# A convolution stem with all its gradients on one core: the order of all engines planned anew, with transfer times by kind and stage

## The chip, the cores and the metric

The kernel runs on one NeuronCore of a Trainium2 chip. The metric is device time in microseconds (us) of one execution. The five engines are TensorE (PE, matmuls), VectorE (DVE), ScalarE (ACT), GpSimd (POOL) and SyncE (SP). SP's and POOL's work here is mostly the issue of DMA transfers, which 16 DMA engines then carry out.

## The reference

A strided convolution over time, a normalisation over time in each channel, a tanh-gelu, and the gradients of everything for a given gradient of the output, all in bfloat16:

```python
def _fwd_reference(x, w, gn_gamma, gn_beta):   # x: 2 x 16000 x 256, w: 31 x 256 x 256
    s = 2
    L = (T - K) // s + 1                        # 7985
    h = jnp.einsum('blc,cd->bld', x[:, 0:s * L:s, :], w[0])
    for i in range(1, K):
        h = h + jnp.einsum('blc,cd->bld', x[:, i:i + s * L:s, :], w[i])
    mu = jnp.einsum('bld->bd', h)[:, None, :] / L
    var = jnp.einsum('bld->bd', (h - mu) ** 2)[:, None, :] / L
    h = (h - mu) / jnp.sqrt(var + 1e-5)
    h = h * gn_gamma[None, None, :] + gn_beta[None, None, :]
    return _gelu(h)

def reference(x, w, gn_gamma, gn_beta, grad_out):
    ...
    _out, _vjp = jax.vjp(_f, x, w, gn_gamma, gn_beta)
    _grads = _vjp(grad_out)
    return (_out0, *[jnp.asarray(_g) for _g in _grads])
```

The outputs are out_0 (the gelu), out_1 (the gradient of x), out_2 (of w), out_3 and out_4 (of gamma and beta).

## The kernel before

The convolution is taken apart twice into three branches each, A, B and C, with sums and differences of phases of x (on DVE) and of taps of w, so that fewer matmuls are needed than 31 taps would ask for. PE's work runs in five stages, in this order of time:

- **F0** and **F1**, the forward convolution of the first and the second image (matmuls of `f_mm`, L736), each in four chunks of time. The sums of x are `tt` in `f_sums` (L694), the results leave the accumulators in `f_evac`.
- **G0** and **G1**, the gradient of x (matmuls of `g_mm`, L1324), again in four chunks for each image. G0 holds the three chunks of the first image and the start of the fourth, G1 the rest. For every chunk `e_load` loads what the gelu's backward pass left (tensors dyd) and the forward result (hd); `e_comp` turns them into the gradient of the convolution's output with two scalings (L1206 for hd, L1208 for dyd), a sum (L1217) and four copies (`spread`, L1226, on ACT); `g_sums` takes the differences `first`, `second` and `third` (all L1277) that the matmuls read. `g_three_b` computes a part once, and an ACT copy (L1351) puts it into the second half of the accumulator, where `g_three_ac` adds to it. `g_seed` (L1385, or `keep`, L831) and `g_evac` (L1395) move accumulators. `dl_turn` transposes the differences by DMA (L549) and stores them to the tensors dld for the last stage. In the same stretch as G0's first half the gelu's backward pass of the second image runs on ACT and DVE (`gelu_unit`: L1096 and L1098, L1101, L1103 and L1105, L1107, L1111, L1122, L1124).
- **W**, the gradient of w (matmuls of `w_mm`, L1528), in nine combinations of branches. Each loads planes of x (`x_raw`, 1 MB each, tensor in_x_dram), sums them (`w_add`, L1496), loads the tensors dld (`d_tile`), and takes sums and differences of pairs (`pair_x`, L1598; `pair_d`, L1614; `leaf_d`, L1699).

Nothing is issued as it is written. Every instruction, matmul group or transfer is handed to `Plan.add` with its engine, an estimated duration, and the memory that it reads and writes; from the latter come its predecessors. After the whole program is written, `order()` gives every entry a due time: the point of PE's own progress at which it is needed, less its duration, less a number from the table `lead` (by kind: stage, function and caller) and one from the table `fine` (by kind and part, the part being the chunk or combination). `listing()` then walks through time with a model of the five engines and of the DMA queues: whenever an engine is free it takes, among the entries that are ready, the one with the earliest due time. `emit()` issues everything in the order of the start times so found, and pins it. So these numbers alone decide in which order each engine runs its queue; each engine executes its queue strictly in this order, and an instruction that waits holds up all behind it.

A transfer enters the model with `dur`, the time of its issue on SP's queue, `dma`, the time that its packets take, and `ns`, the time of one packet, both worked out in `load` and `turn` from its size and the length of its runs:

```python
        pk = 8192 if run >= 4096 else 4096 if eng == "POOL" else run
        np_ = nbytes / pk
        ns = (PKS if out.space == bass.MemoryType.DRAM else PK)[pk]
        add(eng, {"POOL": 0.74, "SP": 0.46 + 0.00016 * np_, "ACT": 0.4}[eng], [out], [in_],
            lambda: e.dma_start(out=out, in_=in_), dma=np_ * ns / 16e3 * 1.03, ns=ns, tp=SH[pk], slack=slack)
```

The duration of an ACT instruction comes from `act(n)`, of a DVE instruction from `dve(n, rate)`, of a matmul from `mmt(n)`.

Of the kernel before, what the change touches and what calls it, by code (L numbers as in the profile page):

```python
# [30 lines left out]
def act(n, extra=0.0):  # L31
    return 0.06 + n * 0.00097 + extra
# [6 lines left out]
class Plan:  # L39
# [3 lines left out]
    def __init__(self, tc):  # L43
# [10 lines left out]
            "F0 f_evac last": 5.0,  # L54
            "F0 f_mm f_leaf": -288.0,
            "F0 f_mm f_outer": -149.5,
            "F0 f_mm f_three_ac": -4.5,
            "F0 f_mm f_three_b": -5.5,
            "F0 f_mm pe_turn": -527.0,
            "F0 f_outer forward": -46.0,  # L60
            "F0 f_seed forward": -48.5,
            "F0 f_three_b forward": -129.5,
            "F0 keep f_evac": 35.5,
            "F0 load conv_stem_kernel": -15.5,
            "F0 load f_evac": 42.5,
            "F0 tt f_sums": -120.5,
            "F0 tt second": 20.5,
            "F0 tt third": -36.0,
            "F0 turn w2_part": -3.0,
            "F0 turn x_load": -8.5,  # L70
            "F0 ve f_seed": -122.5,
            "F0 ve_neg f_seed": 49.0,
            "F0 w_sub f_first": -76.5,
            "F0 w_sum w2_part": -13.5,
            "F1 f_evac last": -106.5,
            "F1 f_mm f_leaf": -335.0,
            "F1 f_mm f_outer": 74.0,
            "F1 f_mm f_three_ac": -8.5,
            "F1 f_mm f_three_b": -75.5,
            "F1 f_three_b forward": -73.0,  # L80
            "F1 gelu_unit gelu_batch": -2.0,
            "F1 load gelu_unit": 23.0,
            "F1 load out0_store": 15.0,
            "F1 tt f_sums": -79.5,
            "F1 tt gelu_unit": -49.5,
            "F1 tt second": -38.0,
            "F1 tt third": -225.5,
            "F1 turn gelu_batch": 56.0,
            "F1 turn gelu_unit": -12.5,
            "F1 turn x_load": 35.5,  # L90
            "F1 w_sub f_again": 4.5,
            "G0 e_comp e_load": 0.5,
            "G0 g_evac last": 1.5,
            "G0 g_mm g_leaf": -24.5,
            "G0 g_mm g_outer": 22.0,
            "G0 g_mm g_three_ac": -0.5,
            "G0 g_mm g_three_b": -7.0,
            "G0 g_three_b input_grad": 4.5,
            "G0 gelu_unit gelu_batch": -7.0,
            "G0 keep g_evac": -281.0,  # L100
            "G0 keep g_seed": -15.0,
            "G0 load dl_turn": 2.5,
            "G0 load e_load": 41.0,
            "G0 load g_evac": 23.5,
            "G0 load gelu_unit": -7.0,
            "G0 spread e_comp": -1.0,
            "G0 tiny elem_finalize": -1.0,
            "G0 tt first": -111.5,
            "G0 tt second": -4.5,
            "G0 tt third": -12.5,  # L110
            "G0 turn dl_turn": 3.5,
            "G0 turn gelu_batch": -12.0,
            "G0 w_sum load_w2": -53.0,
            "G0 w_sum w2_outer": -11.5,
            "G1 cp e_comp": 13.5,
            "G1 e_comp e_load": 13.5,
            "G1 g_evac last": -0.5,
            "G1 g_mm g_outer": -7.5,
            "G1 g_mm g_three_ac": -9.0,
            "G1 g_mm g_three_b": -30.5,  # L120
            "G1 g_three_b input_grad": -66.0,
            "G1 keep g_seed": -132.0,
            "G1 load dl_turn": 11.0,
            "G1 load e_load": -8.0,
            "G1 load g_evac": 12.0,
            "G1 spread e_comp": -1.5,
            "G1 tt first": -1.0,
            "G1 tt second": -17.0,
            "G1 tt third": -86.5,
            "G1 turn dl_turn": 3.5,  # L130
            "G1 zero e_comp": -8.0,
            "W keep w_keep": -5.5,
            "W keep weight_grad": -31.0,
            "W leaf_d weight_grad": 0.5,
            "W load d_tile": -49.5,
            "W load out0_late": 165.0,
            "W load w_done": 3.0,
            "W load w_emit": 24.5,
            "W load weight_grad": 2.5,
            "W load x_raw": 1.0,  # L140
            "W pair_d weight_grad": -3.0,
            "W pair_x weight_grad": 1.0,
            "W turn out0_late": -38.0,
            "W ve w_done": 11.5,
            "W ve weight_grad": -24.0,
            "W w_add weight_grad": 2.5,
            "W w_add x_tile": 8.0,
            "W w_both weight_grad": 11.0,
            "W w_emit weight_grad": -234.0,
            "W w_mm w_leaf": -9.0,  # L150
            "W w_pairs weight_grad": -136.0,
# [3 lines left out]
        self.overlap = {"DVE": 0.084, "ACT": 0.1}  # L155
        self.fine = {
            "F0 f_evac last": {0: -191.0, 1: -57.0, 3: -4.0},
            "F0 f_mm f_outer": {0: 138.5, 2: 14.0},
            "F0 f_mm f_three_ac": {0: -41.0, 1: -74.0, 2: -68.0, 3: -25.5},
            "F0 f_mm f_three_b": {2: 96.5, 3: 55.0},  # L160
            "F0 f_mm pe_turn": {0: -106.0},
            "F0 f_outer forward": {0: 69.5},
            "F0 f_seed forward": {0: -15.0, 3: -58.5},
            "F0 keep f_evac": {1: -5.5, 2: -40.5, 3: -32.5},
            "F0 load f_evac": {0: -85.5, 3: 8.5},
            "F0 load put": {1: 170.5, 3: 1.0},
            "F0 load_gb conv_stem_kernel": {1: -70.0},
            "F0 tt f_sums": {1: 46.0, 3: 20.0},
            "F0 tt second": {0: 77.0, 1: -78.0, 2: 2.0, 3: -60.0},
            "F0 tt third": {0: 60.5, 1: -127.0, 2: 39.0, 3: -34.5},  # L170
            "F0 turn w2_part": {1: 3.0, 3: -18.0},
# [1685 lines left out]
```

## Time and profile before

| | |
|---|---|
| median of 3 runs | 1154.29 us (1152.07 to 1155.96) |
| profiled execution | 1154.13 us, span 1152.4 us |
| PE busy | 1122.5 us (97%), 7652 matmuls |
| DVE busy | 997.9 us (87%), 920 instructions |
| ACT busy | 532.7 us (46%), 817 instructions |
| POOL busy | 125.4 us (11%) |
| longest waits of PE | 4.7 and 4.5 us in the first 23 us, 3.4 us at 655 us, 2.8 us at 1006 us |

The span is the profiled execution from its first to its last instruction; the execution's own time holds 1.73 us more. Since PE is busy for 97% of it, a place matters where PE stands still, and the question at each such place is which engine's instruction it waits for, what stood ahead of that one in its engine's queue, and which transfer in turn held that. In a row of a timeline the numbers are the start in us from the beginning of the span, the duration, the engine, the line, the operation, what it writes and reads, and how many instructions are taken together; in brackets behind it stands the idle time of the engine just before it and what ended it. SPq is SP's queue, in which the issue of transfers is listed.

### The profile page before, as it was taken

To read this page: it belongs to the slowest core of one execution; us is meant where nothing else is said; L and a number is where in the kernel's file an instruction comes from. 1 tells how busy PE (TensorE), PEld (TensorE's weight loads), DVE (VectorE), ACT (ScalarE), POOL (GpSimd) and SP (SyncE) were. 2 spreads that over 40 slices of the span, in tenths; PEclk is the share of its full clock that TensorE was granted. 3 is DMA by queue.
4 is the path that set the end of the run, shared out by engine and by line. 5 is a ranking of instruction groups with operands and counts; after the bars stand their busy time and mean duration, and the time that the engine had idled before them with its cause. 6 is when DMAs were issued, how large, how long until landed. Compare 5 with 4: busy or idle time off the path is not lost. (4 is left out here: it accounts for less than half of the span.)

```text
span 1152.4 us, 18848 instructions
## 1 busy us (share of the span) xinstructions
PE 1122.5 (97%) x7652; PEld 749.9 (65%) x7652; DVE 997.9 (87%) x920; ACT 532.7 (46%) x817; POOL 125.4 (11%) x221
## 2 busy tenths in 40 slices
PE   5999999999999999999999899999999999999998
PEld 3888899877777874444444344444588666656785
DVE  7997787798989997999999787877799998689995
ACT  1354444768776588897744355722211212211200
POOL 0000000000000012232323223232100000000000
PEclk8999999999999999999999999999999999999999
DMA  9476657769795599999888779787997825899484
GB/s 219 69 189 119 167 156 150 171 173 203 189 232 129 203 370 267 278 274 270 225 213 189 154 203 214 201 218 147 297 293 225 305 88 167 303 296 371 146 254 119
DMA packets 345807, 243.57 MB, mean 211 GB/s; under 512 B 233377, under 2 KB 316967, under 8 KB 341543
## 3 DMA queue, kind: packets, MB, share of 16 engines
q1 hardware_dynamic: 338615, 223.47, 72.5%
q0 software_dynamic: 7104, 18.89, 5.9%
q8 instruction: 60, 0.98, 0.4%
q14 instruction: 28, 0.23, 0.1%
HBM read 106.24 MB, written 80.25 MB: 162 GB/s over the span
## 5 line engine op out<-in xcount | busy, mean ns | idle before, releaser
L736 PE MATMUL ps<-arena 128*128 128x256 bf16 (+4 forms) x3460 | 407.8, 281 | 12.4 <-DMA arena<-in_x_dram 5.5
L1324 PE MATMUL ps<-arena 128*128 128x512 bf16 x1872 | 404.5, 377 | 6.9 <-DVE arena L1277 3.4
L736 PEld LDWEIGHTS <-arena 128*128 128x128 bf16 x3460 | 338.9, 99 | 81.0 <-DMA arena<-in_x_dram 5.7
L1324 PEld LDWEIGHTS <-arena 128*128 128x128 bf16 x1872 | 183.5, 98 | 226.8 <-issue 11.4
L1528 PE MATMUL ps<-arena 128*128 128x256 bf16 (+1 forms) x2320 | 311.2, 297 | 6.5 <-DVE arena L1598 4.9
L1528 PEld LDWEIGHTS <-arena 128*128 128x128 bf16 x2320 | 227.5, 98 | 90.3 <-DVE arena L1598 5.7
L831 ACT ACTIVATE arena<-ps 128x1024 f32<-128x1024 f32 x109 | 111.0, 1022 | 262.3 <-PE ps L1528 90.1
L694 DVE TENSOR_TENSOR arena<-arena 128x2080 bf16<-128x2080 bf16 (+8 forms) x126 | 156.5, 1267 | 34.0 <-PE ps L736 33.6
L544 POOL DMA_DIRECT2D dld<-arena x144 | 104.3, 727 | 261.9 <-DMA arena<-arena 248.3
L1111 DVE TENSOR_TENSOR arena<-arena 128x2048 bf16<-128x2048 bf16 (+1 forms) x80 | 95.7, 1196 | 9.6 <-ACT arena L1103 5.3
L1277 DVE TENSOR_TENSOR arena<-arena 128x1032 bf16<-128x1032 bf16 (+1 forms) x126 | 87.5, 725 | 8.7 <-ACT arena L1226 3.3
L1496 DVE TENSOR_TENSOR arena<-arena 128x4096 bf16<-128x4096 bf16 x38 | 86.2, 2286 | 7.4 <-DMA arena<-in_x_dram 3.8
L1385 DVE TENSOR_TENSOR ps<-ps,arena 128x2048 f32<-128x2048 f32 x30 | 68.9, 2296 | 26.0 <-ACT arena L831 14.8
L1395 DVE TENSOR_TENSOR arena<-ps,arena 128x1024 bf16<-128x1024 f32 x64 | 77.0, 1218 | 8.1 <-PE ps L1324 4.8
L851 ACT ACTIVATE arena<-ps 128x512 bf16<-128x512 f32 (+1 forms) x64 | 37.1, 581 | 54.0 <-PE ps L736 53.4
L1630 ACT COPY ps<-ps 128x256 f32<-128x256 f32 x54 | 19.2, 358 | 85.2 <-PE ps L1528 84.1
L553 POOL MEMSET arena<- 128x128 bf16 (+11 forms) x40 | 8.6, 245 | 425.4 <-DVE arena L694 140.0
L1351 ACT COPY ps<-ps 128x512 f32<-128x512 f32 x48 | 27.7, 578 | 46.8 <-PE ps L1324 45.6
L1699 DVE TENSOR_TENSOR arena<-arena 128x4608 bf16<-128x4608 bf16 x16 | 40.6, 2551 | 4.7 <-PE ps L1528 4.7
L806 ACT ACTIVATE arena<-ps 128x512 f32<-128x512 f32 x56 | 29.7, 597 | 32.5 <-DVE ps L816 18.8
L772 ACT ACTIVATE ps<-ps 128x256 f32<-128x256 f32 x75 | 27.6, 369 | 34.7 <-PE ps L736 33.5
L1614 DVE TENSOR_TENSOR arena<-arena 128x2048 bf16<-128x2048 bf16 x36 | 42.8, 1218 | 0.8 <-DMA out_dram<-arena 0.8
(81 smaller groups left out, 717.1 us busy)
## 6 DMA issues: line engine op xcount, KB each, us to landing
arena<-in_x_dram SPq DMA_DIRECT2D x40, 1024.0 KB
dld<-arena POOLq DMA_DIRECT2D x144, 128.0 KB, 3.9
arena<-hd SPq DMA_DIRECT2D x32, 512.0 KB
out_dram<-arena SPq DMA_DIRECT2D x14, 1024.0 KB
arena<-dld SPq DMA_DIRECT2D x18, 640.0 KB
arena<-dld SPq DMA_DIRECT2D x18, 576.0 KB
vl<-arena SPq DMA_DIRECT2D x36, 256.0 KB
arena<-vl SPq DMA_DIRECT2D x9, 1024.0 KB
```

What stands on the lines that cost most here:

```text
L544: lambda: e.dma_start(out=out, in_=in_), dma=np_ * ns / 16e3 * 1.03, ns=ns, tp=SH[pk], slack=slack)
L694: lambda: nc.vector.tensor_tensor(out=o, in0=a, in1=b, op=ALU.add))
L736: yield nc.tensor.matmul(ps[:, dh, cs], lhsT=wt, rhs=mv, start=s0, stop=False, skip_group_check=True)
L831: lambda: nc.scalar.activation(out=out, in_=ps, func=ACT.Copy, scale=scale))
L1111: add("DVE", dve(nf), [o], [a, b_], lambda: V.tensor_tensor(out=o, in0=a, in1=b_, op=op))
L1277: lambda: nc.vector.tensor_tensor(out=o, in0=a, in1=b, op=ALU.subtract))
L1324: yield nc.tensor.matmul(ps[:, e, 0:wide], lhsT=lt, rhs=mv, start=s0, stop=False, skip_group_check=True)
L1385: lambda: nc.vector.tensor_tensor(out=o, in0=x, in1=g, op=ALU.add))
L1395: lambda: nc.vector.tensor_tensor(out=ho[:, :, k, :], in0=ps[:], in1=g, op=ALU.add))
L1496: add("DVE", dve(4096), [o], [a, b], lambda: nc.vector.tensor_tensor(out=o, in0=a, in1=b, op=ALU.add))
L1528: yield nc.tensor.matmul(ps[:, s, c0:c1], lhsT=lt, rhs=mv, start=s0, stop=False, skip_group_check=True)
L1614: add("DVE", dve(2048), [o], [u, v], lambda o=o, u=u, v=v: nc.vector.tensor_tensor(out=o, in0=u, in1=v, op=ALU.subtract))
```

## The change

Three things change in the planner, and no instruction is added, removed or altered: `act()` gets another constant and slope; a new table `pace` multiplies `dma` and `ns` of SP's transfers by a factor for each kind; and all numbers of `lead` and `fine` are replaced.

```diff
 def act(n, extra=0.0):
-    return 0.06 + n * 0.00097 + extra
+    return 0.15 + n * 0.00085 + extra
...
         self.lead = {
-            "F0 f_evac last": 5.0,
-            "F0 f_mm f_leaf": -288.0,
...
+            "F0 f_evac last": -1.0,
+            "F0 f_mm f_leaf": -279.5,
...
+        self.pace = {
...
+            "G0 load e_load": 1.23,
...
+            "G1 load e_load": 1.52,
...
+            "W load x_raw": 1.05,
...
+        }
...
         kind = self.stage + " " + f.f_code.co_name + " " + f.f_back.f_code.co_name
+        if eng == "SP" and dma is not None:
+            dma, ns = (v * self.pace.get(kind, 1.0) for v in (dma, ns))
```

The tables are longer by some rows, so that all lines of the program below them move down by 45: L1277 of before is L1322 now, L1206 is L1251, L544 is L589.

The new numbers move instructions in every stage, on all engines. Three places:

SP's queue in the first chunk of the second image in G1, at about 627 to 647 us of the profile before. Before: two stores of out_1 with transposes of differences between them, the loads of dyd and hd for the first half of the image's second chunk (dyd1_1 and hd1_1), transposes, and the loads for that chunk's second half.

```order
227 L544 DMA out_1_dram<-arena_118 128x4096
228 L549 DMA_TRANSPOSE arena_118<-arena_118 128x4x128 x6
229 L544 DMA out_1_dram<-arena_118 104x4096
230 L544 DMA arena_118<-dyd1_1_73 128x2048
231 L544 DMA arena_118<-hd1_1_65 128x2048
232 L549 DMA_TRANSPOSE arena_118<-arena_118 128x4x128 x8
233 L544 DMA arena_118<-dyd1_1_73 128x2048
234 L544 DMA arena_118<-hd1_1_65 128x2048
```

After, at the same place:

```order
222 L594 DMA_TRANSPOSE arena_118<-arena_118 128x4x128 x15
223 L589 DMA out_1_dram<-arena_118 128x4096
224 L589 DMA arena_118<-hd1_1_65 128x2048
225 L589 DMA arena_118<-dyd1_1_73 128x2048
226 L594 DMA_TRANSPOSE arena_118<-arena_118 128x4x128 x3
227 L589 DMA out_1_dram<-arena_118 104x4096
228 L589 DMA arena_118<-hd1_1_65 128x2048
229 L594 DMA_TRANSPOSE arena_118<-arena_118 128x4x128 x2
230 L589 DMA arena_118<-dyd1_1_73 128x2048
```

The first pair of loads has moved ahead of three of the six transposes and of the store with 104 rows; hd comes before dyd. The load of hd for the second half follows that store.

DVE at the start of G0, at about 416 to 424 us. Before: a `second` and a `first`, a sum of w (L682), the two `third` that G0's first matmuls read (128x2x2x258), then a scaling of hd, a `second`, a scaling of dyd, a `second` and the sum L1217.

```order
293 L1277 TENSOR_TENSOR arena<-arena 128x1032
294 L1277 TENSOR_TENSOR arena<-arena 128x2064
295 L682 TENSOR_TENSOR arena<-arena 128x2048
296 L1277 TENSOR_TENSOR arena<-arena 128x2x2x258 x2
297 L1206 TENSOR_SCALAR arena<-arena,stats 128x2048
298 L1277 TENSOR_TENSOR arena<-arena 128x1032
299 L1208 TENSOR_SCALAR arena<-arena,stats 128x2048
300 L1277 TENSOR_TENSOR arena<-arena 128x1032
301 L1217 TENSOR_TENSOR arena<-arena 128x2048
```

After, at the same place:

```order
296 L1322 TENSOR_TENSOR arena<-arena 128x1032
297 L1322 TENSOR_TENSOR arena<-arena 128x2064
298 L1322 TENSOR_TENSOR arena<-arena 128x1032
299 L1251 TENSOR_SCALAR arena<-arena,stats 128x2048
300 L1322 TENSOR_TENSOR arena<-arena 128x2x2x258
301 L1251 TENSOR_SCALAR arena<-arena,stats 128x2048
302 L1322 TENSOR_TENSOR arena<-arena 128x2x2x258
303 L1253 TENSOR_SCALAR arena<-arena,stats 128x2048
304 L1322 TENSOR_TENSOR arena<-arena 128x1032
```

The sum of w has gone ahead (out of the piece), and of the two `third` the one that stood first now stands last, behind a `second`, two scalings of hd and the other `third`.

DVE in the second chunk of G0, at about 475 to 486 us. Before: an evacuation (L1395), the sum L1217, a `second` (row 360), the gelu's L1101 and L1107 between two evacuations, a scaling of hd, a product L1111, and the `second` of row 367, which PE's `g_leaf` reads.

```order
358 L1395 TENSOR_TENSOR arena<-ps,arena 128x2x512
359 L1217 TENSOR_TENSOR arena<-arena 128x2048
360 L1277 TENSOR_TENSOR arena<-arena 128x1032
361 L1395 TENSOR_TENSOR arena<-ps,arena 128x2x512
362 L1101 SCALAR_TENSOR_TENSOR arena<-arena 128x2048
363 L1395 TENSOR_TENSOR arena<-ps,arena 128x2x512
364 L1107 TENSOR_SCALAR arena<-arena 128x2048
365 L1206 TENSOR_SCALAR arena<-arena,stats 128x2048
366 L1111 TENSOR_TENSOR arena<-arena 128x2048
367 L1277 TENSOR_TENSOR arena<-arena 128x1032
```

After, at the same place; the `second` of before's row 360 is row 373 now, and that of row 367 is row 375:

```order
365 L1146 SCALAR_TENSOR_TENSOR arena<-arena 128x2048
366 L1440 TENSOR_TENSOR arena<-ps,arena 128x2x512
367 L1152 TENSOR_SCALAR arena<-arena 128x2048
368 L1253 TENSOR_SCALAR arena<-arena,stats 128x2048
369 L1251 TENSOR_SCALAR arena<-arena,stats 128x2048
370 L1156 TENSOR_TENSOR arena<-arena 128x2048
371 L1262 TENSOR_TENSOR arena<-arena 128x2048
372 L1156 TENSOR_TENSOR arena<-arena 128x2048
373 L1322 TENSOR_TENSOR arena<-arena 128x1032
374 L1156 TENSOR_TENSOR arena<-arena 128x2048
375 L1322 TENSOR_TENSOR arena<-arena 128x1032
```

Both `second` stand behind scalings, a sum and products that came after them before; on PE the leaf that reads them is issued 36 matmuls earlier than before.

Elsewhere: on ACT at about 434 us the four activations L1096 and L1098 of the first gelu unit now come ahead of a `keep` and a copy L1351; on SP at about 963 us one load of `x_raw` moves up by four places, and the four loads of `d_tile` for combination 5 now come with the two of 2560 columns first and the two of 2304, which PE's first pairs read, last; before, both kinds alternated.

More of the change, by code (lines that the diff above doesn't have):

```diff
@@ L92, in __init__ @@
+            "F1 ve f_seed": -32.5,
+            "F1 ve_neg f_seed": 56.5,
+            "F1 w_sub f_again": -1.5,
+            "F1 zero f_evac": 4.5,
+            "G0 cp e_comp": 12.5,
             "G0 e_comp e_load": 0.5,
[L93 removed]
+            "G0 g_evac last": 2.0,
             "G0 g_mm g_leaf": -24.5,
[L95 to L99, printed above, removed]
@@ L106, in __init__ @@
+            "G0 load dl_turn": 2.0,
+            "G0 load e_load": 41.5,
+            "G0 load g_evac": 26.5,
+            "G0 load gelu_unit": -2.0,
+            "G0 load load_w2": 11.5,
             "G0 spread e_comp": -1.0,
             "G0 tiny elem_finalize": -1.0,
[L108 to L114, printed above, removed]
```

364 lines of the change are left out of this document (202 added, 162 removed).

## The prediction

> **What bounds the kernel now.** I read the page first, then PE's waits, then the windows around the longest of them, then the timelines of the engines that ended these waits.
>
> ```profile
> PE 1122.5 (97%) x7652; PEld 749.9 (65%) x7652; DVE 997.9 (87%) x920; ACT 532.7 (46%) x817; POOL 125.4 (11%) x221
> ```
>
> TensorE (PE) is busy for 1122.5 of 1152.4 us. Its matmuls stay the same, so all that a new order can move is the 29.9 us in which PE stands, and time at a lower clock. PE's waits, as us in total, times and longest:
>
> ```profile
> PE ps L1528 <- DVE arena L1598: 4.9, 3, 2.8
> PE ps L736 <- DVE arena L678: 4.7, 1, 4.7
> PE ps L1324 <- DVE arena L1277: 3.4, 1, 3.4
> PE ps L1324 <- ACT ps L1351: 1.5, 2, 0.9
> PE ps L1324 <- DVE arena L1395: 0.9, 1, 0.9
> ```
>
> L736 is the forward stage, L1324 the input gradient, L1528 the weight gradient. The 4.7 at L736 lies at the start, where the change leaves PE and VectorE (DVE) almost as they were. The others are single places, each behind one instruction of DVE or ScalarE (ACT). The windows (length, then busy us of PE, PEld, DVE, ACT, POOL with instruction counts, PEclk, DMA share, GB/s) show that stage by stage:
>
> ```profile
> core 0: us, PE busy (x) PEld busy (x) DVE busy (x) ACT busy (x) POOL busy (x), PEclk, DMA share, GB/s
> 27.00:420.00 393.00, 392.68 (x3367) 328.88 (x3366) 345.30 (x333) 233.74 (x431) 8.48 (x19) 1.00 0.70 172
> 446.00:530.00 84.00, 81.34 (x382) 37.11 (x380) 79.04 (x85) 69.45 (x81) 25.51 (x45) 1.00 1.05 276
> 530.00:654.00 124.00, 123.91 (x579) 56.55 (x578) 114.32 (x133) 67.66 (x80) 36.41 (x55) 1.00 0.84 211
> 658.00:662.00 4.00, 3.46 (x9) 1.23 (x10) 2.22 (x3) 3.16 (x5) 2.54 (x5) 0.57 0.85 178
> 1010.00:1014.00 4.00, 4.00 (x24) 2.87 (x23) 4.00 (x3) 1.07 (x3) 0.00 (x0) 0.57 1.08 337
> ```
>
> Two things stand here. The forward stage has 0.3 us of idle PE in 393, so nothing can be won there. In the input gradient of the first image (420 to 654) DVE is busy for 94% and 92% of two windows: any DVE instruction put too late there is felt by PE at once. And after the two longest stalls PE's clock is 0.57 of full over 4 us: 0.43 x 4 = 1.7 us more for each.
>
> **The stall at 655 us (place A).** PE, then DVE, then SyncE's queue (SPq):
>
> ```profile
> 658.54 1.89 PE L1324 MATMUL ps<-arena 128*128 128x512 bf16 x4 [3.39 <-DVE arena L1277]
> 649.40 2.30 DVE L1385 TENSOR_TENSOR ps<-ps,arena 128x2048 f32<-128x2048 f32 x1 [1.70 <-ACT arena L831]
> 653.17 0.75 DVE L1208 TENSOR_SCALAR arena<-arena,stats 128x2048 bf16<-128x2048 bf16 x1 [1.48 <-DMA arena<-dyd]
> 655.81 0.81 DVE L1206 TENSOR_SCALAR arena<-arena,stats 128x2048 bf16<-128x2048 bf16 x1 [1.88 <-DMA arena<-hd]
> 657.79 0.69 DVE L1277 TENSOR_TENSOR arena<-arena 128x1032 bf16<-128x1032 bf16 x1
> 626.91 16.64 SPq L549 DMA_TRANSPOSE arena<-arena  x6
> 643.65 0.50 SPq L544 DMA_DIRECT2D out_dram<-arena  x1
> 644.20 0.35 SPq L544 DMA_DIRECT2D arena<-dyd  x1
> 644.59 1.81 SPq L544 DMA_DIRECT2D arena<-hd  x1
> ```
>
> PE needs the difference of L1277 at 657.79. It stands behind two instructions that wait for loads of dyd and hd, and these loads were issued at 644.2 and 644.6, behind six transposes and a store. The change puts both ahead of the last three transposes and of that store, so they can go at about 631, when the third transpose is through; even with the 11 us that hd took here they land at 642. The pair after them now takes the place behind the store. One of its L1206 also stands straight ahead of the L1277, but it is issued at about 645.5, and I expect it to land near 654, a little after the first load behind the store did here (653.1). Then the difference ends at about 655.4 against the 655.2 at which PE comes: a remainder of 0 to 0.5. Gain 3.39 - 0.5 + 1.7 = 4.6.
>
> **The stalls of the weight gradient (places C and D).**
>
> ```profile
> 839.11 10.64 PE L1528 MATMUL ps<-arena 128*128 128x256 bf16 x96 [0.64 <-DVE arena L1609]
> 866.27 0.61 PE L1528 MATMUL ps<-arena 128*128 128x256 bf16 x4 [1.57 <-DVE arena L1598]
> 867.40 2.79 PE L1528 MATMUL ps<-arena 128*128 128x256 bf16 x24 [0.53 <-DVE arena L1598]
> 1009.48 2.81 PE L1528 MATMUL ps<-arena 128*128 128x256 bf16 x15 [2.80 <-DVE arena L1598]
> 989.34 2.29 DVE L1496 TENSOR_TENSOR arena<-arena 128x4096 bf16<-128x4096 bf16 x1 [2.56 <-DMA arena<-in_x_dram]
> 1003.54 4.62 DVE L1496 TENSOR_TENSOR arena<-arena 128x4096 bf16<-128x4096 bf16 x2 [3.23 <-DMA arena<-dld]
> ```
>
> At D the sums of L1496 wait 2.56 and 3.23 us for loads of x, and PE's 2.80 follows. One 1 MB load of x moves up by four places, so the one that the first sum awaits has one load fewer ahead of it. I take its earlier landing as 2.5 us, the wait that it caused (bounds 0 and 2.8); the sums, the loads behind them and PE's matmul all follow. A part stays, since the four loads of dld now end with the two that PE needs: gain 2.5 of 2.80, and 1.2 of the 1.7 of clock: 3.7. At C one sum is put behind five short instructions: of 1.57 + 0.53 about 0.75 stays, the 0.64 goes, and a pair sum put ahead of two differences costs 0.7 four us earlier: gain 1.2. All gains: 4.6 + 3.7 + 1.2 = 9.5 (bounds 2.3 and 12).
>
> On the clock the rows say: 3.39 and 2.80 us of idle PE were each followed by the slow stretch. The Trainium skill (TensorE: Matmul & The Clock Gate, Part 1) lets the clock fall after at least one idle window of about 3.4 us; by that D would save no clock and the forecast would be 1.2 us higher. The 2.80 us row speaks against it.
>
> **What the input gradient loses (place E).** Its beginning, with means of one (ns) from the groups of 396 to 530 us behind the timeline rows:
>
> ```profile
> 420.70 9.56 PE L1324 MATMUL ps<-arena 128*128 128x512 bf16 x43
> 419.46 1.30 DVE L1277 TENSOR_TENSOR arena<-arena 128x1032 bf16<-128x1032 bf16 x2
> 423.27 1.22 DVE L1217 TENSOR_TENSOR arena<-arena 128x2048 bf16<-128x2048 bf16 x1
> L1111 DVE TENSOR_TENSOR arena<-arena 128x2048 bf16<-128x2048 bf16 x25 | 30.5, 1221 | 3.5 <-ACT arena L1103 3.2
> L1277 DVE TENSOR_TENSOR arena<-arena 128x1032 bf16<-128x1032 bf16 (+1 forms) x29 | 21.2, 747 | 2.4 <-ACT arena L1226 2.4
> L1206 DVE TENSOR_SCALAR arena<-arena,stats 128x2048 bf16<-128x2048 bf16 x8 | 6.6, 825 | 0.3 <-DMA arena<-hd 0.3
> L1226 ACT COPY arena<-arena 128x768 bf16<-128x768 bf16 (+1 forms) x32 | 18.4, 615 | 1.5 <-DVE arena L1217 0.8 <-POOL arena L553 0.7
> L1351 ACT COPY ps<-ps 128x512 f32<-128x512 f32 x13 | 7.5, 577 | 1.8 <-PE ps L1324 1.8
> L1098 ACT ACTIVATE arena<-arena,stats 128x1024 bf16<-128x1024 bf16 x10 | 11.9, 1229 | 0.0
> 485.18 0.69 DVE L1277 TENSOR_TENSOR arena<-arena 128x1032 bf16<-128x1032 bf16 x1
> 477.72 22.49 PE L1324 MATMUL ps<-arena 128*128 128x512 bf16 x105
> ```
>
> First, at 420.70 PE now wants the four matmuls that read the first of the two L1277 of 419.46, which ended at 420.1. That L1277 moves behind another two of its kind and two L1206: two L1277 take 1.30, two L1206 about 1.5, so it ends at 422.9. PE waits 2.2. Three groups of four matmuls later (0.86 each) PE needs a copy of L1351. That stands now behind an L1226 which reads L1217's result; L1217 moves back by one L1206, from 424.5 to 425.3, and 0.83 + 0.58 after that is 426.7, against 425.5 for PE: 1.2 more. Together 3.4.
>
> Second, at about 434 four activations (L1096, L1098) move ahead of such a copy: it becomes up to 4.6 us later, on a PE already 3.4 late. I take 1.0 (bounds 0 and 2.4). The wait of 0.6 on L1351 at 453 then goes.
>
> Third, the last row but one: PE's leaf that needs this L1277 (ended 485.9) was the 57th matmul of the 105 in the last row, so at 489.7. It now stands 36 matmuls earlier, and 22.49 / 105 x 36 = 7.7 us: 482.0, plus the delay so far (3.4 + 1.0 - 0.6 = 3.8), 485.8. On DVE the L1277 gets one L1206 more ahead of it, and I add 1.0 for DVE's own waits on a late PE: it ends at 487.6. PE waits 1.8, and is 5.6 late.
>
> Then the waits of 0.9 on L1351 and 0.9 on L1395, at 523 and 525, are covered: 3.8 stay. For 530 to 654, as full and as freely permuted, I take 1.0 (bounds 0 and 4). New stalls of about 2 us lie between 1.57 us, after which the clock stayed at full, and 2.80: 0.9 for the clock (bounds 0 and 3.4). For the forward stage, where 0.3 us of idle PE in 393 shows no slack and many loads and stores move, 1.0 (bounds -0.3 and 2). The rest, the second image and the other combinations, 0.8 (bounds -1 and 2). Losses 3.8 + 1.0 + 0.9 + 1.0 + 0.8 = 7.5. Moved zero stores, POOL's stores and the stores of the first output cost nothing, as none of their landings was waited for; if that cover goes it is a fraction of the 0.8.
>
> **Sum.** The profiled execution took 1154.13 us, a span of 1152.4 and 1.73 around it. 1154.13 - 9.5 + 7.5 = 1152.1. The median of the runs is 0.16 above the profiled one, so 1152.3.
>
> **Rivals.** *The input gradient holds.* DVE's idle time in 420 to 530, or loads that land sooner than I think, cover the new places, and only 1.5 is lost. For: DVE's order was dense before too, and PE lost only 2.4 us in 446 to 530. Against: the first place is counted in DVE's own durations, with no transfer in it. 1154.3 - 8 = 1146.
>
> *The input gradient compounds (slower).* A late PE delays the evacuations (L1395) that DVE has queued ahead of the next differences; DVE then waits on PE, and its 6 to 8% of idle time is used up. Upper bounds: 3.4 + 2.4 at the first two; the leaf's wait at 3.9 (485.9 - 482.0) with no delay before it; two slow stretches of 1.7; 4 in 530 to 654; 2 in the forward stage; less 1.8: 17. It decides once more than 9.5 + 3.5 = 13 is lost. 1154.3 - 9.5 + 16.5 = 1161.
>
> *Loads only change places.* At A the next hd lands as late as the first did (655.7), and with 0.81 + 0.69 the difference ends at 657.2: a stall of 2.0 in place of 3.39, and the slow stretch stays or goes; at D the four dld end as late as before. Gains shrink to 2.5, losses stay: 1159. The rows behind the store at 643.65 speak for it, landing one after the other; that the reordered load is free to go 13 us sooner speaks against. By the Trainium skill (DMA: Bandwidth & Descriptors, Queues, rings and completion order) each DMA engine takes descriptors in ring order, so what moves ahead pushes the rest back; the two landings at A agree.
>
> **How the numbers follow.** Measurement can tell about 0.3%, 3.5 us, from no change: 1150.8 to 1157.8. The forecast has 0.45; its own range is 1148 to 1156, of which 0.30 lies within, 0.13 below, 0.02 above. The gradient that holds has 0.24, all faster; the one that compounds 0.24, all slower; loads that only change places 0.07, 0.04 slower and 0.03 within. Faster 0.37, same 0.33, slower 0.30. From 1143 (the holding case with the upper bound of the gains) to 1161 the range leaves out about 2 in 10.
>
> **What would show it.** Right: no wait on dyd or hd at 650 to 656 and PE's 3.4 us on L1277 gone; the 2.8 us at 1006 under 1 us with no 0.57 clock behind it; new PE waits near 421 (on L1277), 426 (on the copy L1351) and 485 (on L1277), 5 us in all. Wrong: no PE wait over 1 us in 420 to 490 (then about 1146), or over 13 us more idle PE in 0 to 654; or the stalls at 655 and 1006 still there.

## The result and the profile after

The changed kernel took 1157.76 us (median of 12 runs, 1155.89 to 1161.82), the kernel before 1154.22 on the same chip (12 runs, 1149.98 to 1156.95). The ratio is 1.0032, with a 95% interval of 1.0018 to 1.0047: slower by about 0.3%, where 1152.3 was forecast. The profiled execution has a span of 1155.7 us against 1152.4.

PE's work and DVE's are unchanged; PE's waits are not. The first answer below is PE's waits of the changed kernel from 30 to 530 us, the second from 830 us to the end (us in total, times, longest):

```profile
PE ps L1369 <- ACT ps L1396: 4.1, 4, 2.1
PE ps L781 <- DVE ps L861: 2.4, 1, 2.4
PE ps L1369 <- ACT arena L1271: 2.1, 1, 2.1
PE ps L1369 <- ACT ps L876: 1.4, 1, 1.4
PE ps L1369 <- DVE arena L1322: 0.8, 1, 0.8
PE ps L781 <- ACT ps L817: 0.5, 1, 0.5
```

```profile
PE ps L1573 <- DVE arena L1643: 1.7, 3, 0.7
PE ps L1573 <- DVE arena L1659: 0.8, 1, 0.8
PE ps L1573 <- ACT ps L1675: 0.3, 1, 0.3
PE ps L1369 <- DVE ps L1430: 0.3, 1, 0.3
```

From 30 to 530 us PE waits for 11.3 us, where before it waited for 3.0 by the same sum; from 830 us on for 3.1, where it was 6.4. PE's own timeline of after shows the longer waits in square brackets; the windows below it (columns as in the prediction) show the clock:

```profile
393.06 24.60 PE L781 MATMUL ps<-arena 128*128 128x231 bf16 x240 [2.43 <-DVE ps L861]
419.98 1.46 PE L1369 MATMUL ps<-arena 128*128 128x512 bf16 x3 [2.10 <-ACT arena L1271]
429.30 2.76 PE L1369 MATMUL ps<-arena 128*128 128x512 bf16 x12 [0.80 <-DVE arena L1322]
433.34 18.84 PE L1369 MATMUL ps<-arena 128*128 128x512 bf16 x88 [1.28 <-ACT ps L1396]
...
486.41 7.93 PE L1369 MATMUL ps<-arena 128*128 128x512 bf16 x36 [2.12 <-ACT ps L1396]
495.70 4.48 PE L1369 MATMUL ps<-arena 128*128 128x256 bf16 x22 [1.36 <-ACT ps L876]
...
639.82 53.34 PE L1369 MATMUL ps<-arena 128*128 128x512 bf16 x248
...
699.74 10.60 PE L1369 MATMUL ps<-arena 128*128 128x512 bf16 x47 [1.89 <-DVE arena L1322]
...
1014.58 5.63 PE L1573 MATMUL ps<-arena 128*128 128x256 bf16 x50 [0.47 <-DVE arena L1643]
```

```profile
420.00:424.00 4.00, 3.89 (x20) 2.43 (x21) 4.00 (x5) 2.78 (x9) 1.17 (x3) 0.58 0.99 394
1014.00:1018.00 4.00, 3.52 (x33) 3.07 (x33) 3.91 (x4) 1.95 (x5) 0.00 (x0) 1.00 1.08 351
```

Places A and D are mended: PE runs from 639.8 to 693.2 without a wait, 0.47 us are left at D, and the clock stays at 1.00 behind it. The losses are new: two waits that end at 393 and 420 us, the second followed by a clock of 0.58, then six in the input gradient's first 100 us, and 1.89 that end at 700.

The first of them begins on DVE some 20 us earlier. These are rows of the timeline of before, by engine:

```profile
369.07 0.35 SPq L544 DMA_DIRECT2D arena<-vl  x1
...
371.33 2.27 DVE L1111 TENSOR_TENSOR arena<-arena 128x1856 bf16<-128x1856 bf16 x2
...
374.33 1.23 DVE L682 TENSOR_TENSOR arena<-arena 128x2048 bf16<-128x2048 bf16 x1 [0.73 <-DMA arena<-vl]
...
379.11 1.12 DVE L1111 TENSOR_TENSOR arena<-arena 128x1856 bf16<-128x1856 bf16 x1
...
382.97 2.04 ACT L806 ACTIVATE arena<-ps 128x512 f32<-128x512 f32 x4
...
386.88 1.22 DVE L816 TENSOR_TENSOR ps<-arena,ps 128x1024 f32<-128x1024 f32 x1
...
392.93 0.33 SPq L544 DMA_DIRECT2D arena<-dyd  x1
```

And of after:

```profile
365.19 6.25 SPq L594 DMA_TRANSPOSE arena<-in_grad_out_dram  x1
...
371.55 0.53 SPq L589 DMA_DIRECT2D arena<-vl  x1
...
378.23 1.23 DVE L727 TENSOR_TENSOR arena<-arena 128x2048 bf16<-128x2048 bf16 x1 [4.80 <-DMA arena<-vl]
379.38 3.43 DVE L1156 TENSOR_TENSOR arena<-arena 128x1856 bf16<-128x1856 bf16 x3
...
386.05 1.12 DVE L1156 TENSOR_TENSOR arena<-arena 128x1856 bf16<-128x1856 bf16 x1
...
389.71 2.04 ACT L851 ACTIVATE arena<-ps 128x512 f32<-128x512 f32 x4
391.78 1.23 DVE L861 TENSOR_TENSOR ps<-arena,ps 128x1024 f32<-128x1024 f32 x1 [0.35 <-ACT arena L851]
...
401.00 0.32 SPq L589 DMA_DIRECT2D arena<-dyd  x1
```

The sum of w (`w_sum`, L682, now L727) reads a load of vl. Before, two of the gelu's products (L1111) stood ahead of it, and it waited for 0.73 us. After, it stands ahead of them; its load is issued 2.5 us later, and DVE waits for 4.80 with three products queued behind. The gelu unit's last product ends 6.9 us later, ACT's copies for `f_outer` begin 6.7 us later, the difference L861 of `f_seed`, which writes the accumulator that PE needs next, comes 4.9 us later, and PE stands for 2.43.

The wait of 2.10 on the spread L1271 is another matter. The loads of dyd and hd for the gradient are issued 8.1 us later than before, but this chain makes only a part of that. In the run both_back below, in which the chain is broken, the loads are still 4.0 us later than before, behind two loads of vl that the order before issued after them (at 393.79), and PE still waits for the spread:

```profile
390.56 6.29 SPq L589 DMA_DIRECT2D arena<-vl  x2
396.94 0.38 SPq L589 DMA_DIRECT2D arena<-dyd  x1
...
416.58 0.82 PE L1369 MATMUL ps<-arena 128*128 128x512 bf16 x3 [2.31 <-ACT arena L1271]
```

So this wait comes from other parts of the new order ahead of 418 us: with before's order up to there (before_to_418) it is gone. Which engine's queue makes it, no run shows by itself.

### The profile page after: what moved, and what is told of

It reads as the page before. It is cut to its first block, busy times and chain, and to the rows that moved or that the text cites. A ratio compares the mean times of both kernels' runs of the same rounds, so it can differ in the third digit from the quotient of the medians.

```text
span 1155.7 us, 18856 instructions
## 1 busy us (share of the span) xinstructions
PE 1122.2 (97%) x7652; PEld 748.8 (65%) x7652; DVE 998.5 (86%) x920; ACT 530.9 (46%) x817; POOL 131.3 (11%) x221
## 4 chain that ended last, share of the span: by engine, by line
PE 66%; DVE 17%; DMA 7%; SPq 4%; ACT 4%; issue 3%; DVEq 0%; ACTq 0%
PE ps L781 24%; PE ps L1369 22%; PE ps L1573 19%; SPq L594 3%; DVE arena L739 2%; DVE arena L1541 2%; DMA arena<-in_x_dram 2%; DVE arena L1156 2%; DVE ps L1430 1%; DVE arena L723 1%; DVE arena L1643 1%; DVE arena L1659 1%; DMA arena<-dyd 1%; DMA out_dram<-arena 1%; DMA hd<-arena 1%
## 5 line engine op out<-in xcount | busy, mean ns | idle before, releaser
L589 POOL DMA_DIRECT2D dld<-arena x144 | 104.4, 727 | 268.2 <-DMA arena<-arena 234.4
L1322 DVE TENSOR_TENSOR arena<-arena 128x1032 bf16<-128x1032 bf16 (+1 forms) x126 | 89.2, 725 | 8.7 <-PE ps L1369 7.0
L1440 DVE TENSOR_TENSOR arena<-ps,arena 128x1024 bf16<-128x1024 f32 x64 | 77.1, 1217 | 5.0 <-PE ps L1369 5.0
L1146 DVE SCALAR_TENSOR_TENSOR arena<-arena 128x2048 bf16<-128x2048 bf16 (+1 forms) x16 | 35.8, 2237 | 12.6 <-ACT arena L1143 12.6
L1396 ACT COPY ps<-ps 128x512 f32<-128x512 f32 x48 | 27.8, 579 | 35.3 <-PE ps L1369 35.3
```

The costliest lines, as they stand in the source:

```text
L1322: lambda: nc.vector.tensor_tensor(out=o, in0=a, in1=b, op=ALU.subtract))
L1440: lambda: nc.vector.tensor_tensor(out=ho[:, :, k, :], in0=ps[:], in1=g, op=ALU.add))
```

## The experiments

Each run is compared with the kernel before in the same session; for after that ratio is 1.0032. Medians of different sessions are not compared with each other, since the kernel before itself took 1153.9 to 1155.6 us in them. Gains in us are the difference of the medians within a session, or the ratio times 1154 where it says so. In the orders the planner's steps have numbers, and `MOVES` puts step i right behind step j:

```diff
-        for i in self.order():
+        for i in moved(self.order()):
...
+MOVES = ((1237, 870),)
+def moved(order):
+    for i, j in MOVES:
+        order.remove(i)
+        order.insert(order.index(j) + 1, i)
+    return order
```

### Where the forward stage loses

**w_sum_later**: after, with the diff above: the sum of w (1237) goes behind the three products.

> After's order, but the one DVE sum of w (L727) that waits 4.8 us for its load at 373 us is put behind three products L1156 of the gelu unit. Theory 1 (one late load starts a chain): the three products (1.13 us from start to start) use 3.4 of the 4.8 us, everything behind them on DVE comes about 3.4 us earlier, PE's waits of 2.43 us at 390 and 2.10 us at 417 go, and the stretch at half clock behind the second (about 1.5 us) with them: 6 us less, 1151.8. Theory 2 (the prediction's: the loss lies in the order of DVE and ACT inside the input gradient): no change, 1157.8.

Measured: 1154.47, ratio 0.9984 (0.9970 to 0.9999). The PE wait at 390 is gone, as Theory 1 said; that on the spread is not, it is 2.3, at full clock.

**stores_first**: after, with the two stores of the first output (853, 854) ahead of the gelu unit's transfer of dyd (846) that waits for DVE; this frees SP for the transpose and the load of vl. (The expectations call 846 a load, since the function `load` issues it; its row reads dyd<-arena, so it is a store.)

```diff
+MOVES = ((853, 852), (854, 853))
```

> After's order, but on SP's queue the two stores of the first output at 363 us go ahead of the load of hd at 362.7, which waits for its buffer and holds them up (the order that before has there). Theory 1: the stores go at 360, the transposes behind the load end earlier, and the load of w behind these is issued at its earliest, about 369, in place of 371.3: the wait of 4.8 us shrinks to between 1 and 3, and 2 to 6 us come back: 1152 to 1156. Theory 2: no change, 1157.8.

Measured: 1153.96, ratio 0.9991 (0.9975 to 1.0006). DVE's wait on vl falls from 4.80 to 0.59.

**both_back**: after, with both.

```diff
+MOVES = ((1237, 870), (853, 852), (854, 853))
```

> After, with two moves taken back at once: on SP the two stores ahead of the gelu's load that waits, on DVE the sum of w behind three products. Each alone took after from 1157.8 to about 1154. Theory 1 (two links of one chain, so that breaking either breaks it): 1153.5 to 1154.5. Rival (two causes): 1157.8 - 3.3 - 3.8 = 1150.7.

Measured: 1153.44, ratio 0.9993 (0.9980 to 1.0007). No more than either alone: one chain with two links, worth 0.0039 to 0.0048 in the ratio, 4.5 to 5.5 us, each good to about 2 us. The traces show less of it: PE's waits from 30 us to the end sum to 17.0 us in after and to 16.1, 15.2 and 14.9 in these three, since other waits grow, and the low clock of after (1.7 us) is gone in the first two only.

Then the same two places put into before. **load_first** has both, **w_sum_early** only DVE's, **load_alone** only SP's:

```diff
+MOVES = ((846, 845), (853, 846), (854, 853), (1237, 867))
...
+MOVES = ((1237, 867),)
...
+MOVES = ((846, 845), (853, 846), (854, 853))
```

> The order of before with two things of after put in: on SP the gelu's load that waits for DVE stands ahead of the two stores of the first output (and so do the stores wait), and on DVE the sum of w that waits for a load of w stands ahead of three products. In after these two go with a DVE wait of 4.8 us at 373 and a PE wait of 2.4 us at 390, and moving either back gave 3.3 to 3.8 us. Theory 1 (these two places are enough by themselves): the DVE wait on the load of w is over 3 us, PE waits over 1.5 us at about 390, and the time is 1158 to 1161. Theory 2 (in before the load of w waits until 368.8 for PE, later than SP gets to it, so the two hurt only on top of an SP queue and a DVE that are already late in after): DVE waits under 2 us, no PE wait over 0.5 us at 390, 1155 to 1156.5.

> The order of before with one instruction moved: on DVE the sum of w that waits for a load of w stands ahead of two of the gelu's products (three places earlier in the list, as in after). Theory 1 (the place on DVE alone makes the loss): a DVE wait of over 3 us on the load of w at about 370 to 374, a PE wait of about 2 us near 384 or 390, and 1157.5 to 1160. Theory 2 (SP's place is needed as well): no PE wait over 0.5 us between 380 and 420, and 1154 to 1156.

> The order of before with one change: on SP the gelu's load that waits for DVE stands ahead of the two stores of the first output. Theory 1 (DVE's place alone makes the loss): the load of w lands within 0.5 us of 374.1, no PE wait over 0.5 us between 380 and 420, and 1154 to 1156. Theory 2 (SP's place makes it, or a part): 1157 to 1160.

In load_first and w_sum_early the sum of w overtakes three instructions, two products and a sum of x (L694); in after it overtakes the two products alone.

Measured: load_first 1159.41, ratio 1.0033 (1.0016 to 1.0050); w_sum_early 1156.48, 1.0026 (1.0009 to 1.0043), a little under its expected range; load_alone 1155.24, 1.0011 (1.0000 to 1.0022). Rows of w_sum_early:

```profile
373.89 1.22 DVE L682 TENSOR_TENSOR arena<-arena 128x2048 bf16<-128x2048 bf16 x1 [3.80 <-DMA arena<-vl]
...
385.19 10.99 PE L736 MATMUL ps<-arena 128*128 128x231 bf16 x98 [2.01 <-ACT ps L772]
```

One DVE instruction, three places earlier on its engine, makes a DVE wait of 3.80 and a PE wait of 2.01, and costs 2.2 us by the medians, 3.0 by the ratio. Its load lands as in before; nothing but its place is different. SP's order alone shows 1.0 us by the medians, 1.3 by the ratio (the interval reaches 1.0000), and no PE wait there; DVE's wait on vl is 0.8 in it.

### What the gradient's start costs

**before_to_446** takes the order of before on all engines to about 450 us and after's from there on; **before_to_418** does so to 418 us, so that the gradient's start is after's, on top of a forward stage that is before's. The loop runs over a written list:

```diff
-        for i in self.order():
+        for i in ORDERED:
```

> Before's order up to the matmul group that it starts at 450 us, after's order for all the rest. If the stages add up: after's loss of 9.9 us before 446 is gone, all that it gains and loses later stays: 1148. Rival (a late PE covered the later stages): the waits of before at 517 to 525 come back or new ones appear, and less than half comes back: 1153 or more.

> The order of before on every engine up to 418 us (the last step taken from it is the evacuation at 417.5; the gradient's first second, first, thirds and copies come after it), then the order of after to the end. Base: before's order to 450 us gave 1148.5. Theory 1, the mechanism of the forecast (the order of after at the gradient's start is itself too late: the third behind the second and two scalings, 2.2 us; the copy behind the spread, 1.2 us; 0.4 us of evacuations): 2.0 to 3.5 us more than that base, 1150.5 to 1152, with PE waits of about 2 at 421 on L1322 and about 1 at 426 on L1396. Theory 2 (those places cost nothing by themselves; the loss at 385 to 446 comes whole from the lateness that DVE and ACT bring from 360 to 400 us): no PE wait over 0.5 us between 385 and 446, and 1148 to 1149.5.

Measured: before_to_446 1148.54, ratio 0.9940 (0.9922 to 0.9959); before_to_418 1148.62, 0.9935 (0.9915 to 0.9956). Both beat both kernels. By the waits the forecast's mechanism is there; by the time it isn't: before_to_446 has waits of 2.8 and 1.4 later on, and PE's waits from 30 to 530 us sum to 4.9 in it and to 5.7 in before_to_418. PE's timeline of before_to_418, and of **to_418_third**, where the two thirds and the copy go back to before's places:

```diff
+# in before_to_418's list: 1270 behind 1245, 1490 behind 1270, 1283 behind 1492
```

> The order of before up to 418 us and of after behind it (1148.6 us, with PE waits of 2.1 on L1322 at 422 and 1.1 on L1396 at 426), and in it three moves at the gradient's start: on DVE the two thirds stand behind the sum of w again and ahead of a second and two scalings, on ACT the copy that PE waits for stands ahead of the spread. Theory 1 (the forecast's terms of 2.2 and 1.2 for these places are real, and PE keeps what it wins): both waits fall under 0.3 us and the time is 2.5 to 3.5 us lower, 1145 to 1146. Rival (PE comes to the next evacuations and copies earlier and waits there instead): 1147.5 to 1149.

```profile
422.14 2.76 PE L1369 MATMUL ps<-arena 128*128 128x512 bf16 x11 [2.08 <-DVE arena L1322]
425.98 18.84 PE L1369 MATMUL ps<-arena 128*128 128x512 bf16 x87 [1.08 <-ACT ps L1396]
```

```profile
422.32 1.89 PE L1369 MATMUL ps<-arena 128*128 128x512 bf16 x8 [0.40 <-ACT arena L896]
425.70 1.89 PE L1369 MATMUL ps<-arena 128*128 128x512 bf16 x8 [1.50 <-DVE arena L1262]
428.25 17.16 PE L1369 MATMUL ps<-arena 128*128 128x512 bf16 x79 [0.66 <-DMA arena<-vl]
```

Measured: to_418_third 1148.30, ratio 0.9944 (0.9923 to 0.9966), no gain; the 2.5 us of Theory 1 would need a ratio near 0.991. The waits of 2.08 and 1.08, almost to the digit the 2.2 and 1.2 of the forecast, are gone, and 0.40, 1.50 and 0.66 stand in their place on others; PE's waits from 30 to 530 us sum to 5.7 in both. What these instructions leave to PE, others take, mostly DVE's next ones.

**four_back** does the same in after's own order, on top of both_back.

```diff
+MOVES = ((1237, 870), (853, 852), (854, 853), (1270, 1210), (1490, 1270), (1283, 1492))
```

> After with the two moves of the run before this one taken back, and with the thirds ahead of one second-and-scaling pair less, and the copy ahead of the spread, at the gradient's start. PE waits at 418 to 430 were 2.3 on the spread, 1.1 on L1322 and 1.1 on L1396 when one of the two was taken back. Theory 1 (the forecast's places cost 1.1 each in after's own order): the last two fall to under 0.5 together, and the time is 1.5 to 2 us under the run before. Rival (they are covered by the wait on the spread, or turn up later): within 0.7 us of it.

Measured: 1153.07, ratio 0.9994 (0.9981 to 1.0007), as both_back. The waits on L1322 and L1396 are 0.79 and 0.56 here, 0.80 and 1.28 in both_back, and one of 1.12 on a `keep` is new.

### The gains, alone and together

**loads_only** is before with place A's two loads ahead of three transposes and the store, **x_raw_only** with place D's load of x four places earlier, **two_moves** both, **three_moves** also puts two leaf differences of the weight gradient behind what PE needs first at place C:

```diff
+MOVES = ((2062, 2148), (2061, 2062))
...
+MOVES = ((2979, 2973),)
...
+MOVES = ((2062, 2148), (2061, 2062), (2979, 2973))
...
+MOVES = ((2062, 2148), (2061, 2062), (2979, 2973), (2771, 2780), (2785, 2781))
```

> The order of before with one thing changed: on SP the loads of dyd and hd for the gradient's next part (issued at 644 us in before) stand ahead of the last three transposes and the store; DVE's, ACT's and PE's orders are as before. Theory 1 (place A is set by the time at which these two loads are issued): the loads go at about 631 us, PE's 3.4 us on L1277 at 655 falls under 0.5 us and the 0.57 clock behind it goes, 4.6 to 5.2 us less than before. Rival (loads only change places: what is pushed back, three transposes and the pair of loads behind the store, is then waited for): a PE wait of 2 us stays at 650 to 660, and the time is at most 2 us under before.

> The order of before with one thing changed: on SP one 1 MB load of x for the weight gradient stands four places earlier, right behind the first of its group. Theory 1 (place D is set by the turn of that load): PE's wait of 2.8 us on L1598 at 1006 falls under 1 us and the 0.57 clock behind it goes, 3.7 to 4.7 us less than before. Rival (the load takes the rings' time from the four dld loads that PE's sums need as well, so the sum of the four ends as late): a wait of 1.5 to 2.8 us stays and the time is within 1.5 us of before.

> The order of before with five moves in all and nothing else: on SP the two loads of place A ahead of three transposes and a store, on SP the one load of x of place D four places earlier, on DVE two leaf differences of the weight gradient's second combination behind the pair sums and pair differences that PE needs first (place C). Alone, the first gave 1150.1 and the second 1152.1 where before gave 1155.4. Theory 1 (the three places are apart in time, and what PE wins at one is kept to the end): 5.2 + 3.3 + about 1.2 less than before, 1145.7, faster than every order measured so far. Rival (what one place wins, the next gives back, as when two orders were joined in four pieces): 1149 to 1151.

> The order of before with the moves at A (two loads) and D (one load of x) alone; with the third one, at C, they gave 1148.8, and the trace there has PE waits of 3.9 us at 870 to 910 that before does not have. Theory 1 (A and D add up, and the move at C cost 2 us by what it put behind it): no PE wait over 1 us at 870 to 910, and 1155.3 - 5.2 - 3.3 = 1146.8. Rival (A and D do not add up): 1148.5 to 1150.

Measured: loads_only 1150.13, ratio 0.9949 (0.9930 to 0.9969), 5.2 us; x_raw_only 1152.05, 0.9980 (0.9959 to 1.0001), 3.3 us by the medians and 2.3 by the ratio, though the interval just touches 1; two_moves 1146.15, 0.9930 (0.9910 to 0.9949), 7.7 us of the 8.5 that the two add up to by the medians, 0.0070 of 0.0071 by the ratios; three_moves 1148.76, 0.9950 (0.9931 to 0.9968). The loads of A in loads_only, from SP's timeline:

```profile
629.33 0.58 SPq L544 DMA_DIRECT2D arena<-hd  x1
629.95 1.41 SPq L544 DMA_DIRECT2D arena<-dyd  x1
```

No PE wait is left there from 650 to 664, and none in x_raw_only from 990 to 1020. PE's waits of three_moves from 870 to 910 us, where two_moves has none:

```profile
PE ps L1528 <- DVE ps L1638: 1.5, 2, 0.8
PE ps L1528 <- DVE arena L1594: 1.5, 1, 1.5
PE ps L1528 <- DVE arena L1598: 0.9, 2, 0.5
```

My own move at C made 3.9 us of new waits behind it; with what it saves, PE's waits from 830 us on sum to 6.3 in three_moves and to 3.7 in two_moves. The ratio is 0.0020 higher, 2.3 us, though the two intervals overlap. The lowest ratio of all belongs to before with three SP loads moved; before_to_418 (0.9935) can't be told from it.

### Two joins, and two halves of the change

**four_pieces** takes before to 610 us, after to 672, before to 810, after to the end; **before_to_490** takes before to 490 us and after from there.

> Before's order to about 610 us, after's to 672, before's to 810, after's to the end: only the pieces in which after lost less. If they add up: 5.1 less at 655, 1.2 at 830 to 910, 4.6 at 1006, 0.5 more at the end: 1154.2 - 10.4 = 1143.8. Rival (gains depend on what ran before them): above 1148.

> The order of before up to 490 us (the last step is the copy at 489.8), then the order of after. Before's order to 450 us gave 1148.5, with PE waits of 2.8 us on the copy L1396 and 1.4 us on the keep L876 between 446 and 490. Theory 1 (these 4.2 us belong to the order of after in 450 to 490): they fall to the 0.6 us that before shows there, and the time is 1144.5 to 1145.5. Rival (before's own waits of 2.6 us in 490 to 530, or a join of two orders that do not fit, come in their place): 1147 to 1150.

Measured: four_pieces 1155.01, ratio 0.9999 (0.9987 to 1.0011); before_to_490 1151.03, 0.9969 (0.9949 to 0.9988). Neither added up. In four_pieces a load of dyd stands where before had it (613.6), and the scaling that needs it where after has it:

```profile
613.60 0.77 SPq L589 DMA_DIRECT2D arena<-dyd  x1
...
619.41 0.75 DVE L1253 TENSOR_SCALAR arena<-arena,stats 128x2048 bf16<-128x2048 bf16 x1 [4.22 <-DMA arena<-dyd]
...
623.22 6.99 PE L1369 MATMUL ps<-arena 128*128 128x512 bf16 x23 [7.65 <-DVE arena L1440]
```

That is the pattern of 373 us again: DVE waits for a load, and PE pays for what is queued behind. In before_to_490 a PE wait of 7.2 on L1440 appears at 500 us; I haven't followed its cause.

**tables_alone** has after's tables of due times with before's costs, **times_alone** after's costs with before's tables.

```diff
-    return 0.15 + n * 0.00085 + extra
+    return 0.06 + n * 0.00097 + extra
...
-            dma, ns = (v * self.pace.get(kind, 1.0) for v in (dma, ns))
+            dma, ns = (v * 1.0 for v in (dma, ns))
```

> After's two tables of due times, with before's costs: the old constant and slope for ACT and no factors on SP's transfers. Theory 1 (the tables were chosen with the new costs and fit only those): the order is another than after's in most stages, and the time is over 1162. Rival (the tables carry the order, and the costs only shift it a little): within 3 us of after, 1155 to 1161.

> After's costs (ACT's new constant and slope, the factors on SP's transfers) with before's two tables of due times. Theory 1 (costs nearer to the transfers make a better plan whatever the tables are): under 1154. Theory 2 (before's tables were chosen for before's costs, and with others the plan loses that choice): over 1160.

Measured: 1223.31, ratio 1.0587 (1.0560 to 1.0614), and 1245.08, 1.0782 (1.0751 to 1.0813). Neither the new costs nor the new due times make a good order by themselves: here costs and due times are one set.

## Why the prediction was wrong, step by step

**Place A: right.** Gain 4.6 forecast. The wait of 3.39 and 1.7 of clock are gone (5.1), and the move alone gave 5.2. The wait is steady: 3.17 to 3.32 in the runs that leave A as it was.

**Place D: right in mechanism, in size partly by luck.** 3.7 forecast; 2.80 and 1.7 of clock against a rest of 0.47 make 4.0, and the load alone gave 3.3 by the medians, 2.3 by the ratio. The 2.80 and the clock are those of one execution: in loads_only, load_alone and w_sum_early, which leave D as it was, the wait is 2.20, 2.10 and 1.81 at full clock, in load_first 2.15 with the low clock behind it. **Place C: right in size**, 1.2, not wait by wait: between 838 and 907 us 0.64 + 0.58 + 1.57 + 0.53 became 0.81 + 0.68 + 0.52, 1.3 less. All gains: 10.4 by these rows, 9.5 forecast.

**"For the forward stage ... 1.0 (bounds -0.3 and 2)": the step that failed.** It measured 2.43 + 2.10 + 1.7 of clock (0.42 x 4 us) = 6.2. I had read PE's 0.3 us of idle time as the room that the stage has, and bounded the term without following one moved instruction. The trace of before held what was needed for the 2.43: DVE's wait of 0.73 on vl, with two products of 1.13 ahead of it that the change puts behind. 0.73 + 2.3 is a DVE wait of 3.0, on a DVE whose gelu chain ends in sums that PE waits for; in w_sum_early, where a sum of x is overtaken too, the same count gives 4.0 and the trace 3.80. The chain of this one place and SP's order behind it is worth 4.5 to 5.5 us by the ratios, more than the net loss of 3.5. The prediction also put the moved stores of the first output at nothing, as none of their landings was waited for. What counted was their place on SP's queue: moved back, they gave 0.0041 in the ratio, 4.7 us. The 2.10 and the clock behind it are not of this chain, and what makes them stays open. Nor is 6.2 all: before_to_418, which exchanges only the order ahead of 418 us, lies 0.0097 under after in the ratio, about 11 us, and I can't assign the rest.

**The start of the gradient: right in sum, wrong as a mechanism.** Forecast 3.8 from 420 to 530 us. The four rows shown from 429 to 496 sum to 5.6, and with two small ones PE waits 6.24 there, against 2.67 before: 3.6. The waits on L1322 and L1396 came at the places named, as 0.80 and 1.28; with before's forward stage, where PE comes earlier, they are 2.08 and 1.08. At 485 it was the copy L1396 (2.12) and a `keep` (1.36), not the difference L1322 (1.8 forecast). But a price per place was the wrong picture: to_418_third took the first two away and won nothing.

**The rest: near in sum, not in place.** 530 to 654 has no PE wait (1.0 forecast). Before 700 a difference stands behind a sum that waits for ACT, 1.89, inside a term of 0.8. PE's waits and the clock together account for a net loss of 1.7 (10.4 gained; 8.3 + 1.7 lost to 530 us and 2.1 at 654 to 700), the span for 3.3; I can't assign the other 1.6.

**Rivals.** "The gradient compounds" was nearest in sign, but its mechanism isn't what happened: evacuations behind a late PE didn't set it off; the loss lay mostly ahead of the gradient. "Loads only change places" fell with loads_only and with after's own rows at A and D.

## What to carry to other kernels

For each instruction that waits for a transfer and moves earlier on its engine, add the time of what it overtakes to its wait in the old trace, and follow who is queued behind it; do this in the stages too where the bounding engine never stands, since that only says that they are just in time. A wait row of PE prices a stall, not an order: undoing stalls of 2.08 and 1.08 us moved them on in to_418_third, where DVE is busy for 91% of the time from 418 to 530 us, and ACT for 90% in the first 28 us of it. And a small repair of the old order, three loads moved where the trace showed a wait (ratio 0.9930), beat planning everything anew (1.0032).

## What was unexpected in the hardware

The clock after a short stall isn't set by its length alone. both_back and four_back have the same stall of 2.31 us on the spread at 415 us, then one of 0.75; the windows over it read, for both_back and then for four_back:

```profile
416.00:420.00 4.00, 2.66 (x15) 1.85 (x16) 4.00 (x4) 3.31 (x12) 0.56 (x2) 0.82 1.00 387
420.00:424.00 4.00, 4.00 (x33) 3.52 (x32) 4.00 (x7) 0.65 (x2) 2.67 (x4) 0.75 0.81 256
```

```profile
416.00:420.00 4.00, 1.87 (x14) 1.34 (x15) 4.00 (x5) 4.00 (x12) 0.00 (x0) 1.00 0.96 343
420.00:424.00 4.00, 4.00 (x43) 3.95 (x41) 4.00 (x6) 0.75 (x4) 3.23 (x5) 1.00 0.87 300
```

One falls, the other doesn't. After's 2.10 was followed by half clock, its 2.43 and 2.12 were not; nor was 3.17 in x_raw_only, while before's 2.80 and 3.39 were. From 30 us on, in all traces but those of tables_alone and times_alone, 4 of the 16 stalls of 2.0 to 2.9 us were followed by half clock, and 4 of the 5 of 3.17 to 3.39. The Trainium skill (TensorE: Matmul & The Clock Gate, Part 1) lets the clock fall after at least one idle window of about 3.4 us, and calls that window free-running. The free-running part agrees with two outcomes for one stall; the threshold doesn't, as 2.10 and 2.31 us were enough. So the 0.9 us that the forecast set down for the clock is a chance, not a price: 0 or 1.7 for a stall of 2 to 3 us.

A transpose on SP's queue held it for 6.25 us in after (365.19). Its row in before, and in load_alone, where two stores are issued right ahead of it:

```profile
361.02 2.78 SPq L549 DMA_TRANSPOSE arena<-in_grad_out_dram  x1
```

```profile
362.41 5.93 SPq L549 DMA_TRANSPOSE arena<-in_grad_out_dram  x1
```

Two stores right in front make the same instruction hold the queue for twice as long, before anything behind it is issued: 5.93 to 6.36 us in the four traces with that order. With the store of dyd between them and the transpose it is 4.47 and 4.70 (both_back, stores_first), and where the stores go 4 us earlier 2.78. Why, the runs don't show.
